# From batch 2 on, attention runs on 64x64 array tiles without the non-causal quarter, one output pass per batch

## Chip, cores and metric

The kernel runs on one core of one Trainium2 chip. The metric is the device time of one execution in microseconds (us). Three runs of the kernel before gave 292.82, 293.95 and 294.68 us; their median is 293.95 us.

## What is computed

The reference, cut to its core (8 batches, 8 heads, 576 positions, head size 64; then 4608 tokens, model size 512, hidden size 2048):

```python
scores = q @ k.transpose(0, 1, 3, 2) / sqrt(64)
gamma = 1 - 2 ** (-5 - head)
D = where(i >= j, gamma ** (i - j), 0)            # causal decay
attn = (scores * D) @ v
x = attn.transpose(0, 2, 1, 3).reshape(4608, 512)
h = x @ w_in
out = gelu_tanh(h) @ w_out
```

## The kernel before

Attention is computed in chunks: each batch has four chunks of 128 positions (512 in all) and a "tail" of 64. For a chunk the kernel computes scores against the same chunk's keys (`score`, line 376), multiplies them by a causal mask (`masks`, L387), and multiplies by the values (`av`, L453). What came before the chunk enters through a running 64x64 state per head: `state` (L399) forms k-transposed times v of a chunk, `scan` (L416) decays and adds it on VectorE (DVE), `spread` (L430) copies the result on ScalarE (ACT) into a block-diagonal weight tile (`tbd`, for the tails `tbt`), and `past` (L436) multiplies that with the queries. The decay factors are put into q and k when these are cast to f16 on GpSimd (POOL, `cast`, L256); v is cast on ACT. `put` (L466) copies a chunk's output from its PSUM bank into `xT`, on ACT.

The second half is an ordinary two-layer network: `up` (L474) makes 512 tokens' hidden activations, 16 steps of four 512-column matmuls, each followed by a GELU on ACT; `prod` (L646) makes the output in 14 steps of eight 256-column matmuls, by seven products of sums of blocks, whose sums are made on DVE (`act_sums` L634, `after` L673). For the last two of the nine token blocks (`WIN`), the hidden layer uses such sums too.

The order is written out by hand. The outer loop at L990 runs over token blocks t = 0 to 8; block t < 8 is the 512 chunk positions of batch t, block 8 holds the eight tails. A block has 30 steps; steps 0 to 15 are `up` and 16 to 29 are `prod`. After step u the events registered with `at(t, u, f)` run, and these are the attention of batch t + 1 and the casts of batch t + 2. Batches 0 and 1 are handled apart: their attention (`score2` L324, `state2` L353, `av2` L365) already uses four 64x64 tiles of the array, on pairs of heads and chunks. From batch 2 on the loop at L946 places, in block t, for batch b = t + 1:

- at step 9 (11 for t = 2, 3): scores and masks of chunks 0 and 1, and in t = 3, 4, 6, 7 those of a pair of tails (`scores`, L917);
- at step 15: `outs` (L928), that is `past`, `av` and `put` of chunks 0, 1 and the tails, with the state of chunks 2, 3; then the scores of chunks 2, 3;
- at steps 17 and 19: the masks of chunks 2, 3; at 16 and 25 `later` (scan and spread) of chunks 2 and 3;
- at step 24: `outs` of chunks 2, 3, with the state of the next batch's chunks 0, 1, whose `later` runs at steps 0 and 1 of the next block.

In t = 1 these stand at steps 16 (state), 21, 23, 25 and 28. The first `up` of block t + 1 reads all four chunks of batch t + 1 in `xT`, so all its `put`s must be done by then. Steps 16 to 23 also hold the casts of batch t + 2 (loop at L966): k and q on POOL, v on ACT, each as its 256 KB load lands, the v of chunk 3 last, at step 23. After them `turn_dma` (L305) transposes k and q by DMA; the transposed tile `tt` is read by the scores of the next block. All loads, transposes and most stores are issued by one queue, that of SyncE (SP), in program order; `load` (L91) issues one DMA for 128 positions of one of q, k, v, and `load_tails` (L81) two DMAs of 64 positions for a pair of tails.

PSUM has eight banks, which the kernel hands out itself: `bank` takes the first of a queue of spare ones, `drop` appends one at the end.

The tile shapes in the profile: `score` multiplies 64 rows by 128 columns of the array, `av` and `state` 128 rows by 64 columns; so two such matmuls (the two heads of a pair) can be in the array at once. `score2`, `state2` and `av2` use 64 rows by 64 columns, four at once.

Of the kernel before, what the change touches and what calls it, by code (L numbers as in the profile page):

```python
# [20 lines left out]
def kernel(  # L21
# [9 lines left out]
    nc = tc.nc  # L31
# [34 lines left out]

    def drop(t):
        spare.append(home.pop(id(t))[0])
# [22 lines left out]
    def load(b, key, c):  # L91
# [8 lines left out]
        else:  # L100
# [3 lines left out]
            )  # L104
        att[b]["raw"][key, c] = t
# [57 lines left out]
    ip = const.tile([128, 4], I32, name="ip")  # L163
    nc.gpsimd.iota(ip[:, 0:2], pattern=[[1, 2]], base=-64, channel_multiplier=2)
    nc.gpsimd.iota(ip[:, 2:4], pattern=[[0, 2]], base=-64, channel_multiplier=1)
# [3 lines left out]
    ps5 = const.tile([128, 8], F32, name="ps5")  # L169
    nc.vector.tensor_copy(out=ps5[:, 0:4], in_=ip)  # L170
    for s, m in ((slice(0, 2), 128.0), (slice(3, 4), 64.0)):
        nc.vector.tensor_scalar(out=ps5[64:128, s], in0=ps5[64:128, s], scalar1=m, scalar2=None, op0=ALU.subtract)
    nc.vector.tensor_scalar(out=ps5[:, 4:8], in0=ps5[:, 0:4], scalar1=-1.0, scalar2=None, op0=ALU.mult)
    lp = const.tile([128, 64], F32, name="lp")
    sc = const.tile([128, 64], F32, name="sc")

    def pairs(x, n):
        return x[:, 16 * n : 16 * n + 16].rearrange("p (n j l) -> p n j l", j=2, l=2)

    lg = lgr.rearrange("p (n l) -> p n l", l=2).unsqueeze(2).to_broadcast([128, 4, 2, 2])  # L180
    for n in range(2):
        pj = ps5[:, 4 * n : 4 * n + 2].unsqueeze(1).unsqueeze(3).to_broadcast([128, 4, 2, 2])
        nc.vector.tensor_tensor(out=pairs(lp, n), in0=lg, in1=pj, op=ALU.mult)
        nc.vector.tensor_tensor(
            out=lp[:, 32 + 16 * n : 48 + 16 * n].rearrange("p (x h) -> p x h", h=8),
            in0=ps5[:, 4 * n + 2 : 4 * n + 4].unsqueeze(2).to_broadcast([128, 2, 8]),
            in1=lgr.unsqueeze(1).to_broadcast([128, 2, 8]), op=ALU.mult,
        )
    lq = lp.rearrange("p (g n x) -> p g n x", g=2, n=2)[:, :, 0]
    nc.vector.tensor_scalar(out=lq, in0=lq, scalar1=math.log(scale), scalar2=None, op0=ALU.add)  # L190
    nc.scalar.activation(out=sc, in_=lp, func=AF.Exp)
    sp = {key: sc[:, 16 * n : 16 * n + 16].rearrange("p (n l) -> p n l", l=2) for n, key in enumerate("qk")}
    sc = sc[:, 32:64].rearrange("p (s h) -> p s h", h=8)
# [7 lines left out]
    cm = const.tile([128, 128], F32, name="cm")  # L201
    tm = const.tile([128, 128], F32, name="tm")
# [11 lines left out]
    def chunk_masks():  # L214
        for m in (cm, tm):
            nc.gpsimd.memset(m, 1.0)
            nc.gpsimd.affine_select(
# [699 lines left out]
    def scores(t, c, tails=None):  # L917
        b = t + 1
        if b < B:
            score(b, c), score(b, c + 1)  # L920
# [163 lines left out]
```

## Time and profile before

| what | value | where from |
|---|---|---|
| median of 3 runs | 293.95 us | runs |
| lowest, highest run | 292.82, 294.68 us | runs |
| profiled execution, first to last instruction | 291.2 us, clock 1.000 | page (it gives no other time of its own) |
| PE matmul starts of block 2 / 3 / 4 / 5 / 6 / 7 | 84.55 / 114.31 / 144.76 / 175.22 / 204.98 / 235.18 us | timeline |
| `ret<-st` masks on DVE, 128x512 | 680 ns, 48 of them | groups |
| `xT<-xs` puts on ACT, 128x512 | 591 ns, 36 of them | groups |

A line of the timeline has the start in us, the length, the engine, the source line, the operation, the output and input tiles, their shapes, the number of instructions merged, and in brackets the idle time before it with what ended it. PE stands for TensorE's matmuls, with array rows and columns in use ahead of the shape. Lengths of matmuls overlap: a small one takes about 0.2 us from start to end, while the next starts a few ns later, so costs on PE are taken from one start to the next.

### The profile page before, as it was taken

Reading aid. Unit: us, or ns where it says so; the run is one execution under the profiler, and the core shown is the slowest. Engines: PE = TensorE matmul, PEld = TensorE weight load, DVE = VectorE, ACT = ScalarE, POOL = GpSimd, SP = SyncE. Lnnn points to the kernel's source line nnn. Section 1 sums busy time; section 2 is a strip of 40 time slices with the busy share of each in tenths; the row PEclk is TensorE's granted clock in tenths of the full one; section 3 lists DMA queues with packets and bytes.
Section 4 is the critical chain, followed back from the end, with each engine's and each line's share of the span. In section 5 each row is a group of like instructions: output and inputs, shape, how many; then the busy total and the mean of one; then the engine's idle time right before and its main releaser. Section 6 shows DMA issues by size and latency. Waiting matters only on the chain.

```text
span 291.2 us, 7390 instructions
## 1 busy us (share of the span) xinstructions
PE 280.6 (96%) x3028; PEld 208.4 (72%) x3028; DVE 204.2 (70%) x409; ACT 169.2 (58%) x320; POOL 100.5 (35%) x129
## 2 busy tenths in 40 slices
PE   6989998999999999999999999999999999999993
PEld 2568886888874687468845884488548887887783
DVE  5797998656864875477548834774489968974863
ACT  5278755896249545965396547664666258507810
POOL 4588869910760085008500740058030000000000
PEclk9999999999999999999999999999999999999999
DMA  7999999999989999999898979999951030003013
GB/s 196 308 367 360 379 294 240 245 235 179 224 168 243 227 204 194 254 229 199 169 234 204 229 155 239 224 202 157 265 106 38 2 144 3 0 24 122 3 36 108
DMA packets 139585, 53.95 MB, mean 185 GB/s; under 512 B 118048, under 2 KB 131360, under 8 KB 139552
## 3 DMA queue, kind: packets, MB, share of 16 engines
q1 hardware_dynamic: 138960, 52.97, 81.4%
q8 instruction: 23, 0.38, 0.5%
q10 hardware_dynamic: 592, 0.52, 0.5%
q14 instruction: 10, 0.08, 0.1%
HBM read 36.70 MB, written 9.44 MB: 158 GB/s over the span
## 4 chain that ended last, share of the span: by engine, by line
PE 81%; DMA 6%; POOL 5%; SPq 4%; DVE 1%; ACT 1%; issue 1%; POOLq 0%
PE hp L480 26%; PE opB L665 13%; PE opA L665 10%; PE opC L665 8%; PE hp L501 5%; DMA ld<-in_moe_w_in_dram 4%; PE hB L574 3%; SPq L96 3%; PE xs L459 3%; PE st L383 3%; POOL w_out_sb L771 2%; DMA ld<-in_q_dram 2%; PE hC L574 2%; PE xs L450 2%; PE opD L665 1%; PE us L408 1%
## 5 line engine op out<-in xcount | busy, mean ns | idle before, releaser
L480 PE MATMUL hp<-xT,w_in_sb 128*128 128x512 f16 x352 | 79.0, 379 | 0.0
L486 ACT ACTIVATE gT<-hp 128x512 f16<-128x512 f32 x88 | 50.1, 600 | 20.7 <-PE hp L480 20.1
L480 PEld LDWEIGHTS <-w_in_sb 128*128 128x128 f16 x352 | 34.0, 98 | 38.2
L665 PEld LDWEIGHTS <-gT 128*128 128x128 f16 x576 | 54.8, 98 | 8.9 <-issue 0.8
L665 PEld LDWEIGHTS <-s 128*128 128x128 f16 x432 | 42.1, 98 | 5.0
L642 DVE TENSOR_TENSOR s<-gT 128x512 f16<-128x512 f16 x36 | 15.6, 434 | 29.8 <-ACT gT L486 23.5
L665 PE MATMUL opA<-w_out_sb,gT 128*128 128x256 f16 x288 | 36.0, 273 | 0.4 <-ACT w_out_sb L771 0.3
L392 DVE TENSOR_TENSOR ret<-st,cm 128x512 f16<-128x512 f32 x48 | 30.1, 680 | 3.6 <-PE st L383 3.6
L469 ACT CAST xT<-xs 128x512 f16<-128x512 f32 x36 | 19.2, 591 | 18.7 <-PE xs L459 15.6
L501 PE MATMUL hp<-xT,w_in_sb 128*128 128x256 f16 x256 | 29.0, 273 | 0.0
L434 ACT CAST tbd<-ws 64x256 f16<-64x256 f32 x48 | 19.3, 403 | 15.3 <-DVE ws L425 14.7
L275 POOL TENSOR_TENSOR ck<-ld,sc 128x512 f16<-128x512 f32 x24 | 25.0, 1040 | 7.7 <-DMA ld<-in_k_dram 7.7
L978 POOL COPY gate<-s 128x1 f16<-128x1 f16 x5 | 0.9, 188 | 76.5 <-DVE s L646 76.5
L275 POOL TENSOR_TENSOR cq<-ld,sc 128x512 f16<-128x512 f32 x24 | 26.2, 1090 | 2.1 <-DMA ld<-in_q_dram 1.8
L501 PEld LDWEIGHTS <-w_in_sb 128*128 128x128 f16 x256 | 24.6, 98 | 3.1
L665 PE MATMUL opB<-wt,gT 128*128 128x256 f16 x224 | 26.8, 273 | 0.0
L262 ACT CAST cv<-ld 128x512 f16<-128x512 f32 x23 | 13.7, 618 | 18.9 <-DMA ld<-in_v_dram 18.8
L508 ACT ACTIVATE gT<-hp 128x512 f16<-128x512 f32 x32 | 18.3, 602 | 3.2 <-PE hp L501 3.0
L679 DVE TENSOR_TENSOR k<-k,opB 128x512 f32<-128x512 f32 x17 | 11.6, 685 | 12.0 <-PE opB L665 11.0
L425 DVE TENSOR_TENSOR ws<-vs,gt 128x256 f32<-128x256 f32 x24 | 18.2, 760 | 1.1
L665 PE MATMUL opB<-wt,s 128*128 128x256 f16 x144 | 17.4, 273 | 0.0
L665 PE MATMUL opC<-wt,s 128*128 128x256 f16 x144 | 17.2, 273 | 0.0
(122 smaller groups left out, 409.1 us busy)
## 6 DMA issues: line engine op xcount, KB each, us to landing
ld<-in_q_dram SPq DMA_DIRECT2D x32, 256.0 KB, 5.3
ld<-in_k_dram SPq DMA_DIRECT2D x32, 256.0 KB, 5.2
ld<-in_v_dram SPq DMA_DIRECT2D x32, 256.0 KB, 5.5
out_dram<-ost SPq DMA_DIRECT2D x16, 512.0 KB, 3.8
ld<-in_moe_w_in_dram SPq DMA_DIRECT2D x16, 256.0 KB, 5.9
ld<-in_moe_w_out_dram SPq DMA_DIRECT2D x16, 256.0 KB, 5.8
lt<-in_k_dram SPq DMA_DIRECT2D x8, 128.0 KB, 4.7
lt<-in_q_dram SPq DMA_DIRECT2D x8, 128.0 KB, 4.3
```

Of the source, the lines that this page charges most:

```text
L275: eng.tensor_tensor(out=dst.rearrange("p (h d) -> p h d", d=D), in0=raw.rearrange("p (h d) -> p h d", d=D), in1=sc[:, s0].unsqueeze(2).to_ ...
L392: nc.vector.tensor_tensor(out=r.rearrange("p (n i) -> p n i", i=128), in0=t.rearrange("p (n i) -> p n i", i=128), in1=(cm if b < PAIR else ...
L425: nc.vector.tensor_tensor(out=w, in0=uc, in1=gt, op=ALU.mult)
L434: cp(out=(tbd[b % 2][r, c, :, r] if c < NC - 1 else tbt[b % NT4][r, :, r]), in_=w[r])
L469: nc.scalar.copy(out=xT[:, g0 : g0 + 2], in_=xs.rearrange("p (n g t) -> p g n t", n=HP, g=2))
L480: nc.tensor.matmul(hp.rearrange("p (g t) -> p g t", t=TL), w_in_sb[:, ct, 128 * fc : 128 * fc + 128], xT[:, o : o + TB // TL, ct, :], star ...
L486: nc.scalar.activation(out=gT[t][:, fc].rearrange("p i n -> p (i n)"), in_=hp, func=AF.Gelu_apprx_tanh)
L501: nc.tensor.matmul(hps[n][:, 256 * x : 256 * x + 256].rearrange("p (g t) -> p g t", t=TL), w_in_sb[:, ct, 128 * (fs[n] + x) : 128 * (fs[n] ...
L508: nc.scalar.activation(out=gT[t][:, f : f + 2, 2 * u : 2 * u + 2, :].rearrange("p f i n -> p f (i n)"), in_=hp.rearrange("p (f n) -> p f n ...
L574: nc.tensor.matmul(pb[:, 256 * i : 256 * i + 256].rearrange("p (g t) -> p g t", t=TL), w(kt, i), x(kt), start=(new and i == kt == 0), stop ...
L642: nc.vector.tensor_tensor(out=s["1"], in0=a21, in1=a22, op=ALU.add)
L665: nc.tensor.matmul(op[tag][:, HD * u : HD * u + HD], lhs(f), rhs[:, f], start=(new and f == 0), stop=(f == NH - 1), skip_group_check=True,)
```

## The change

From batch 2 on, `score` and `av` work on 64x64 tiles of the array. A chunk's scores are cut in halves of 64 keys: the first 64 keys meet all 128 queries, the last 64 keys only the last 64 queries; the quarter in which keys are later than queries is not computed. One pass (`first`) has the matmuls with 128 columns and the other those with 64. To let the two chunks of a pair use different halves of the array in a pass, the halves of k and v of odd chunks are loaded in exchanged order, by two DMAs of 64 positions each, where one DMA of 128 was. The mask tile is 192 wide per pair of heads and a mask instruction handles 384 columns where it handled 512. The tails get the same treatment (`score_tails`, `av_tails`: no scores between the two tails of a pair).

`state` of a batch is made as 64 matmuls on 64x64 tiles in two passes (batch 2: `state_whole`, 32 on 128x64).

The order changes too. The state of all chunks and the scores of chunks 2, 3 are made together at step 15 (`middle`), with the tails' outputs; `later` runs at steps 16, 18, 20, 22; the outputs of all four chunks are made together at step 24 (`outs`; in t = 1 at step 28), with four `put`s after them. Between the passes stands `turn_over`, a four-column matmul on a 64x64 tile into a bank that is taken anew each time: in the program as built, the second and third of them in `outs`, and the first score matmul of the second bank pair in `middle`, wait on PE's own semaphore for the `turn_over` before. Program counts, before and after: 3028 and 3659 matmuls; 24 DMAs more on SP's queue.

The diff, cut (left out: the widened tables of decay factors that the casts use, more buffers for `ret`, and removed lines of the functions printed above):

```diff
+    def turn_over(n):
+        t = ps.tile([128, 512], F32, tag=f"p{n}", name="turn", bufs=1)
+        nc.tensor.matmul(t[0:64, 0:4], ident[0:64, 0:64], ident[0:64, 0:4], start=True, stop=True)
+
...
-        else:
+        elif key == "q" or c % 2 == 0:
             nc.sync.dma_start(
                 out=t.rearrange("p (h d) -> p h d", d=D),
                 in_=src[b, :, 128 * c : 128 * c + 128, :].rearrange("h s d -> s h d"),
             )
+        else:
+            for n in range(2):
+                r0 = 128 * c + 64 - 64 * n
+                nc.sync.dma_start(
+                    out=t[64 * n : 64 * n + 64].rearrange("p (h d) -> p h d", d=D),
+                    in_=src[b, :, r0 : r0 + 64, :].rearrange("h s d -> s h d"),
+                )
...
-    cm = const.tile([128, 128], F32, name="cm")
-    tm = const.tile([128, 128], F32, name="tm")
+    cm = const.tile([128, 192], F32, name="cm")
+    tm = const.tile([128, 64], F32, name="tm")
...
     def chunk_masks():
+        def causal(x, r, i0, n, base):
+            nc.gpsimd.affine_select(
+                out=x[0:r, i0 : i0 + n], in_=x[0:r, i0 : i0 + n], compare_op=ALU.is_ge, fill=0.0, base=base,
+                pattern=[[1, n]], channel_multiplier=-1,
+            )
+
         for m in (cm, tm):
             nc.gpsimd.memset(m, 1.0)
...
+        causal(cm, 128, 0, 64, 64), causal(cm, 128, 64, 128, 64)
+        causal(cm, 64, 0, 128, 0), causal(cm, 64, 128, 64, 0)
+        causal(tm, 128, 0, 64, 64), causal(tm, 64, 0, 64, 0)
 
...
-            s0 = {"q": 0, "k": 2}[key] + (b >= PAIR)
+            s0 = 1 if b >= PAIR else 2 if key == "k" and c % 2 else 0
...
+    def mm(out, lhsT, rhs, start, stop):
+        nc.tensor.matmul(out, lhsT, rhs, start=start, stop=stop, skip_group_check=True)
+
+    def piece(o, first):
+        w = 128 if first else 64
+        return o if first else 1 - o, w, 0 if o == 0 else 64 if first else 128
+
+    def score(b, g):
+        for x in range(2):
+            st = [bank("st") for _ in range(2)]
+            for p in (2 * x, 2 * x + 1):
+                for first in (True, False):
+                    for o in range(2):
+                        h, w, i = piece(o, first)
+                        i += 192 * (p % 2)
+                        for r in range(2):
+                            mm(
+                                st[r][hv(h), i : i + w], att[b]["tt"][hv(r), 0, 4 * (2 * g + o) + p, hv(h)],
+                                tq(b, 2 * g + o, p)[hv(r), 128 - w : 128], True, True,
+                            )
+            att[b]["st", g, x] = st
+
+    def masks(b, g, x):
+        for k, t in enumerate(att[b].pop(("st", g, x))):
+            r = sb.tile([128, 512], F16, tag="ret", name="ret", bufs=8)
+            nc.vector.tensor_tensor(
+                out=r[:, 0:384].rearrange("p (n i) -> p n i", n=2), in0=t[:, 0:384].rearrange("p (n i) -> p n i", n=2),
+                in1=cm.unsqueeze(1).to_broadcast([128, 2, 192]), op=ALU.mult,
+            )
+            drop(t)
+            att[b]["ret"][g, k, x] = r
+
+    def score_tails(b):
         st = [bank("st") for _ in range(2)]
         for p in range(HP):
...
+            for n in range(2):
+                for hl in range(2):
+                    nc.tensor.matmul(
+                        st[hl][hv(n), 64 * p : 64 * p + 64], att[b]["tt"][hv(hl), 0, p, hv(n)],
+                        tq(b, 0, p)[hv(hl), hv(n)], start=True, stop=True,
+                    )
+        for hl, t in enumerate(st):
+            r = sb.tile([128, 512], F16, tag="ret", name="ret", bufs=8)
             nc.vector.tensor_tensor(
-                out=r.rearrange("p (n i) -> p n i", i=128), in0=t.rearrange("p (n i) -> p n i", i=128),
-                in1=(cm if b < PAIR else tm).unsqueeze(1).to_broadcast([128, 4, 128]), op=ALU.mult,
+                out=r[:, 0:256].rearrange("p (n i) -> p n i", n=4), in0=t[:, 0:256].rearrange("p (n i) -> p n i", n=4),
+                in1=tm.unsqueeze(1).to_broadcast([128, 4, 64]), op=ALU.mult,
             )
             drop(t)
-            att[b]["ret"][c, hl] = r
+            att[b]["ret"][hl] = r
 
     def col(c, p, hl):
         return slice(512 * c + 128 * p + 64 * hl, 512 * c + 128 * p + 64 * hl + 64)
 
-    def state(b, *cs):
+    def state(b, first):
         a = att[b]
-        us = bank("us")
-        for n, c in enumerate(cs):
+        if first:
+            a["us"] = [bank("us") for _ in range(2)]
+        for g in range(2):
+            for p in range(HP):
+                for o in range(2):
+                    h, c = hv(piece(o, first)[0]), 2 * g + o
+                    for hl in range(2):
+                        i = 256 * g + 64 * p
+                        mm(
+                            a["us"][o][hv(hl), i : i + 64], a["k"][h, col(c, p, hl)], a["v"][h, col(c, p, hl)],
+                            first and g == p == 0, not first,
+                        )
+        if not first:
+            for c in range(NC):
+                a["U", c] = (a["us"][c % 2], c // 2, c >= 2)
+
+    def state_whole(b):
+        a = att[b]
+        us = [bank("us") for _ in range(2)]
+        for c in range(NC):
             for p in range(HP):
                 for hl in range(2):
...
+                    i = 256 * (c // 2) + 64 * p
+                    mm(us[c % 2][hv(hl), i : i + 64], a["k"][:, col(c, p, hl)], a["v"][:, col(c, p, hl)], True, True)
+            a["U", c] = (us[c % 2], c // 2, c >= 2)
 
...
     def past(b, c):
         xs = bank("xs")
         att[b]["xs", c] = xs
...
+        if c == 0:
+            return
+        for p in range(HP):
+            nc.tensor.matmul(
+                xs[:, 128 * p : 128 * p + 128], tbd[b % 2][:, c - 1, p, :], tq(b, c, p),
+                start=(p == 0), stop=True, skip_group_check=True,
+            )
+
+    def av(b, g, first):
         a = att[b]
         for p in range(HP):
-            for hl in range(2):
+            for o in range(2):
+                h, w, i = piece(o, first)
+                i += 192 * (p % 2)
+                c = 2 * g + o
+                for hl in range(2):
+                    mm(
+                        a["xs", c][hv(hl), 128 * p + 128 - w : 128 * p + 128],
+                        a["v"][hv(h), col(c, p, hl)], a["ret"][g, hl, p // 2][hv(h), i : i + w],
+                        first and c == p == 0, not first,
+                    )
+
+    def past_tails(b, banks):
+        xs = [bank("xs") for _ in range(banks)]
+        att[b]["xs"] = [xs[0], xs[-1]]
+        for n in range(2):
+            for p in range(HP):
+                o = 128 * p + 64 * n
                 nc.tensor.matmul(
...
+                    att[b]["xs"][n][:, o : o + 64], tbt[(b - PAIR + n) % NT4][:, p, :],
+                    tq(b, 0, p)[:, 64 * n : 64 * n + 64],
+                    start=(p == 0 and (n == 0 or banks > 1)), stop=True, skip_group_check=True,
                 )
+
+    def av_tails(b, *ns):
+        a = att[b]
+        for p in range(HP):
+            for n in ns:
+                for hl in range(2):
+                    mm(
+                        a["xs"][n][hv(hl), 128 * p + 64 * n : 128 * p + 64 * n + 64],
+                        a["v"][hv(n), col(0, p, hl)], a["ret"][hl][hv(n), 64 * p : 64 * p + 64], False, True,
+                    )
+
+    def put_tails(b, banks):
+        xs = att[b].pop("xs")
+        g0 = GM + b - PAIR
+        if banks == 1:
+            nc.scalar.copy(out=xT[:, g0 : g0 + 2], in_=xs[0].rearrange("p (n g t) -> p g n t", n=HP, g=2))
+            drop(xs[0])
+            return
+        for n in range(2):
+            nc.scalar.copy(
+                out=xT[:, g0 + n], in_=xs[n].rearrange("p (n g t) -> p g n t", n=HP, g=2)[:, n]
+            )
+            drop(xs[n])
 
     def put(b, c):
         xs = att[b].pop(("xs", c))
-        g0 = 8 * (b % 2) + 2 * c if b < PAIR else GM + b - PAIR
+        g0 = 8 * (b % 2) + 2 * c
         nc.scalar.copy(out=xT[:, g0 : g0 + 2], in_=xs.rearrange("p (n g t) -> p g n t", n=HP, g=2))
         drop(xs)
 
...
+    def middle(b, tails):
+        x = PAIR + tails if tails is not None else None
+        if x:
+            past_tails(x, 1)
+            av_tails(x, 0)
+        state(b, True)
+        turn_over(spare[2])
+        score(b, 1)
+        if x:
+            av_tails(x, 1)
+        state(b, False)
+        if x:
+            put_tails(x, 1)
+
+    def outs(b):
+        for c in range(NC):
+            past(b, c)
+        n = spare.popleft()
+        av(b, 0, True)
+        turn_over(n)
+        av(b, 1, True)
+        turn_over(n)
+        av(b, 0, False)
+        turn_over(n)
+        av(b, 1, False)
+        spare.append(n)
+        for c in range(NC):
+            put(b, c)
+
+    def last_tails(x):
+        past_tails(x, 2)
+        av_tails(x, 0, 1)
+        put_tails(x, 2)
+
+    at(1, 16, lambda: state_whole(2))
     for t in range(1, B):
         b, tl = t + 1, TP.get(t)
...
         if b == B:
+            at(t, 9, lambda x=PAIR + tl: score_tails(x))
+            at(t, 15, lambda x=PAIR + tl: last_tails(x))
             continue
+        s0, s1 = (21, 25) if t == 1 else (11 if t in (2, 3) else 9, 15)
+        at(t, s0, lambda b=b: (score(b, 0), masks(b, 0, 0), masks(b, 0, 1)))
+        if tl is not None:
+            at(t, s0, lambda x=PAIR + tl: score_tails(x))
         if t == 1:
-            at(t, s1, lambda t=t, b=b: scores(t, 2))
+            at(t, s1, lambda b=b: score(b, 1))
+            um, ul, o1 = (25, 25), (17, 18, 19, 20), 28
         else:
...
+            at(t, s1, lambda b=b, tl=tl: middle(b, tl))
+            um, ul, o1 = (17, 19), (16, 18, 20, 22), 24
+        for x, u in enumerate(um):
+            at(t, u, lambda b=b, x=x: masks(b, 1, x))
+        for c, u in enumerate(ul):
+            at(t, u, lambda b=b, c=c: later(b, c))
+        at(t, o1, lambda b=b: outs(b))
 
```

## The prediction

> **What bounds the kernel now.** First the page: how busy each engine is, and the share of the DMA engines over 40 slices.
>
> ```profile
> PE 280.6 (96%) x3028; PEld 208.4 (72%) x3028; DVE 204.2 (70%) x409; ACT 169.2 (58%) x320; POOL 100.5 (35%) x129
> DMA  7999999999989999999898979999951030003013
> ```
>
> PE is the bound: 96% busy, and from 55 us on the list of waits names none of PE. But the second row matters as much: the DMA engines are full until about slice 28 (205 us). So I read PE's timeline for what attention costs (block t = 2), then ACT's at a block's end.
>
> ```profile
> 95.00 0.62 PE L383 MATMUL st<-tt 64*128 64x128 f16 x16
> 95.55 3.63 PE L480 MATMUL hp<-xT,w_in_sb 128*128 128x512 f16 x16
> 99.02 0.39 PE L450 MATMUL xs<-tt,tbd 128*128 128x128 f16 x4
> 99.33 0.64 PE L459 MATMUL xs<-ret,cv 128*64 128x128 f16 x16
> 99.80 0.42 PE L408 MATMUL us<-cv,ck 128*64 128x64 f16 x16
> 100.15 0.62 PE L383 MATMUL st<-tt 64*128 64x128 f16 x16
> 100.71 1.92 PE L665 MATMUL opA<-w_out_sb,gT 128*128 128x256 f16 x16
> ...
> 108.58 0.61 PE L450 MATMUL xs<-tt,tbd 128*128 128x128 f16 x8
> 109.12 0.64 PE L459 MATMUL xs<-ret,cv 128*64 128x128 f16 x16
> 109.59 0.42 PE L408 MATMUL us<-cv,ck 128*64 128x64 f16 x16
> 109.94 0.28 PE L665 MATMUL opA<-w_out_sb,gT 128*128 128x256 f16 x1
> ```
>
> From start to next start, attention takes 0.55 + 1.69 + 1.36 = 3.60 us of the 29.76 us of this block. Two parts hide in it. Single starts in the trace show pairs of matmuls 56 ns apart at 128 columns and 32 ns at 64; and each change of the array's shape shows a gap of about 0.15 us between starts, so about 0.10 more than the pace. One block has 7 such changes.
>
> Batch 1 already runs on four 64x64 tiles, and prices the new form:
>
> ```profile
> 54.23 0.45 PE L359 MATMUL us<-cv,ck 64*64 64x64 f16 x32
> 54.51 0.62 PE L332 MATMUL st<-tt 64*64 64x128 f16 x32
> ```
>
> 32 matmuls of 64 columns take 0.28 us to the next start (single starts: four together every 32 ns), and 32 of 128 columns come by fours every 56 ns. A 64-column four thus costs 57% of a 128-column four, not half.
>
> ACT at the end of block t = 3:
>
> ```profile
> 137.32 0.62 ACT L262 CAST cv<-ld 128x512 f16<-128x512 f32 x1 [1.29 <-DMA ld<-in_v_dram]
> 142.63 0.62 ACT L262 CAST cv<-ld 128x512 f16<-128x512 f32 x1 [4.69 <-DMA ld<-in_v_dram]
> 143.15 1.07 ACT L469 CAST xT<-xs 128x512 f16<-128x512 f32 x2
> ```
>
> The two `put`s had their bank ready at about 140.2 us, but stood on ACT behind the cast of the last v load, which landed at 142.6. They end at 144.2; the next block's first `up` starts at 144.76. In t = 2 it is the same (cast at 112.08, `put`s from 112.60, `up` at 114.31). The slack is 0.5 to 0.7 us.
>
> **The change part by part.** The sum is made against the profiled execution, whose span is 291.2 us; the median of the runs, 293.95, lies 2.75 above it, and I add these 2.75 at the end.
>
> *Scores and outputs.* Per batch, scores were 16 pairs at 56 ns = 0.90 us; they become 8 fours at 56 and 8 at 32 = 0.70. Outputs the same. Together -0.38 us per batch. Skipping a quarter saves 21%.
>
> *State.* 16 pairs at 32 ns become 16 fours at 32: nothing.
>
> *Changes of shape.* From 7 to 6 per block (scores 2, `middle` 2, `outs` 2): -0.10.
>
> *The turn_overs.* No row shows one. Four a block; one uses one tile for four columns. Bounded by the rows: below by 0.01 (the starts inside a four lie 3 to 4 ns apart), above by a change of shape and a full drain each, 0.3. The waits on PE's own semaphore matter more: a 64-column matmul takes 193 ns to its end and DVE follows PE's end by about 45 ns, so the next one can start about 0.25 us after the last. Between the first two lie 4 fours of 128 columns (0.22 us: no wait), between second and third 4 fours of 64 (0.13: wait 0.10), in `middle` 0.18 (wait 0.05). With 0.02 each for the four and 0.02 for refilling the array, I take 0.25 a block; ends 0.05 and 1.2. The Trainium skill (TensorE: Matmul & The Clock Gate, section "Single matmul latency") would give a lone four-column matmul (398 + 4) / 2.4 = 168 ns, an estimate by that page; with 45 ns it would make the waits about 0.03 shorter each.
>
> So a block saves 0.38 + 0.10 - 0.25 = 0.23 us. A pair of tails (t = 3, 4, 6) saves 0.07 more: scores 4 pairs of 128 become 4 fours of 64 (-0.10), outputs 4 pairs of 128 become 8 pairs of 64 (+0.03). In t = 7, tails alone save 0.20.
>
> *Masks.* 680 ns at 512 columns and 420 for a 256-column DVE operation give about 0.55 at 384: DVE gains 1 us a batch, off the path. In t = 6 DVE runs without a gap from 218.7 to 230.6, and two more scans (1.2 us) now stand there before the one that `past` needs. Counted through, that scan ends at 229.7 and its spread (0.82) at 230.5, `past` of chunk 3 wants it at about 230.4: I take 0.2, ends 0 and 0.8.
>
> *Loads.* 24 more DMAs on SP, which holds all loads and transposes. Behind them wait the casts on ACT and POOL, then the transposes. The nearest row is the tails' loads, the same two DMAs of 64 positions: an issue takes 0.63 us against 0.57 for a whole load when nothing holds it, but the queue is 4 to 5 us ahead of the engines, and what counts is landing. In t = 3 and 5 the tails' pairs landed 1.09 us apart on average, whole loads mostly 1.0 to 1.2. I take 0; ends -0.1 and +0.2 per pair, 16 pairs until the last v of block 3. POOL's new masks (8 instructions for 5 of 0.14 to 0.31, so +0.8) end 2 us before the transposes at 62.15: nothing.
>
> *Four puts at the block's end.* ACT's `put`s follow each other by 0.48, the last takes 0.58. Four end 2.02 us after the first starts. Two of four used to be done at step 15.
>
> Now block by block, as the shift of the next block's first matmul:
> - t = 1: state +0.25 (all four chunks at once), scores -0.20, `outs` at step 23 gone (-1.29): `outs` begins at 81.06, `past` of 12 takes 0.76, `av` with its turns 0.93. The first bank is complete at 82.7, the `put`s end at 84.72. PE alone would be ready at 83.7. It waits 1.05: start 84.75 instead of 84.55, +0.2.
> - t = 2: PE ready at 84.75 + 29.76 - 0.23 = 114.28; ACT: 112.60 + 2.02 = 114.62, and 0.05 to PE. Start 114.67, +0.36.
> - t = 3: PE ready at 144.82; ACT 143.15 + 2.02 + 0.05 = 145.2. Start 145.2, +0.44.
> - t = 4: ACT's last v cast is at 171.58, four `put`s end at 174.2, `up` at 175.4: no wait. -0.30: +0.14. t = 5: -0.23: -0.09. t = 6: +0.26 (half of its batch's state was made in t = 5), -0.30, +0.2: +0.07. t = 7: -0.20: -0.13.
>
> The span is 291.07, the time **293.8 us**: no change. What PE gains up to block 4 is spent waiting for the loads, which are full.
>
> **The rivals.**
> 1. *Loads slip (slower).* If a split pair lands 0.2 us later than a whole load, the v of block 3 lands 3.2 us later, and block 4 starts 3.6 late; after it 0.57 is gained: a span of 294.3, 297.0 us. One per cent is passed from 0.19 us a pair. For it: ten tenths of DMA. Against: the tails' pairs. 12%.
> 2. *Turn_overs drain the array (slower).* At 0.3 each plus waits a block loses 0.7 instead of gaining 0.23: with six such blocks and the waits for ACT within them about +4 us, 298. Against: 64x64 stages with waits of PE on itself run without gaps today. 6%.
> 3. *Matmuls cost by the piece (slower).* If a 64-column matmul on a 64x64 tile took what one on 128x64 takes (0.35 us / 16 = 22 ns), the 128 of a batch would take 2.8 us, not 1.0: +10.7 us, 304. Against it the row at 54.23: 9 ns each. 2%. The Trainium skill (TensorE: Matmul & The Clock Gate, "Wait — 56ns, not 53.3ns?") has a floor of about 25 ns from start to start however few columns: that would speak against this change, +13 us by its figure; here the trace disagrees, with starts 3 to 4 ns apart on different tiles.
> 4. *The gain arrives (faster).* Turns at 0.05 a block and no waiting for `put`s: -0.7 in t = 1, -0.45 or -0.55 in t = 2 to 5, -0.25, -0.2: -3.1, so 290.8. It needs the last v a microsecond earlier than today's 142.6; nothing in the change moves it. 6%.
>
> **The numbers.** Forecast 74%, its own range 292.4 to 295.6: below with turns at 0.05 (-0.9 from the span) and the 0.6 by which runs differ; above with turns at 0.6 a block and the loads at +0.05 a pair. For 8 in 10 the range reaches to 1 and 4 in part: 292.1 to 297.0. One per cent (2.9 us) is about what a measurement here can tell. Faster by more: 5%, rival 4. Slower by more: half of 1, and 2 and 3: 14%. Within: 81%.
>
> **What would show it.** Blocks 2, 3 and 4 begin at 84.8, 114.7 and 145.2, PE idle ahead of the first `hp` for 1.05, 0.4 and 0.4 us, released by the ACT `put`; four `put`s in a row behind the last v cast. The scores' 32 matmuls take 0.45 us to the next start, not 0.55; `outs` 1.7. A block without a wait is 0.2 us shorter (5: 29.5). It is wrong if the last v lands later than 142.6 by a microsecond, or if the turns show gaps of over 0.1 us.

## The result: 3.2% slower

The changed kernel takes 302.21 us (median of five runs, 302.0 to 304.78); the kernel before took 292.93 us beside it (five runs, 292.34 to 294.68). The ratio is 1.0318, 95% interval 1.0274 to 1.0361. The forecast was 293.8 us. Of `e1`, `g1` and `h1` below, some executions (one of four, five of ten, one of twelve) were over 1.5% longer than the fastest of the same kernel, and the ratios leave those out; the median of all ten of `g1` is 298.33 us.

The page of the changed kernel, in the profiled execution (span 302.9 us, its own time 304.78): how busy each engine is, then the granted clock and the DMA share over 40 slices.

```profile
PE 282.9 (93%) x3659; PEld 207.8 (69%) x3659; DVE 195.3 (64%) x410; ACT 171.3 (57%) x321; POOL 101.5 (34%) x132
...
PEclk9999999999999999599999999999999999999999
DMA  7999999999999999999999979999992020003013
```

PE is busy for 2.3 us more than before (282.9 against 280.6) while the span is 11.7 us longer: most of the loss is waiting, and part of the 2.3 is one slice at a lower clock. DMA is full from slice 2 to slice 30 with one dip (slice 24), where before it also dipped at slices 12, 20 and 22 and fell off a slice earlier.

PE's timeline around blocks 2 and 3 of the changed kernel; the brackets hold the idle time and what ended it:

```profile
86.44 10.52 PE L570 MATMUL hp<-xT,w_in_sb 128*128 128x512 f16 x48 [0.93 <-ACT xT L559]
98.47 0.54 PE L396 MATMUL st<-tt 64*64 64x128 f16 x32 [1.52 <-DMA tt<-cq]
...
112.90 0.40 PE L502 MATMUL xs<-tt,tbd 128*128 128x128 f16 x4 [0.77 <-ACT tbd L494]
...
122.77 13.04 PE L570 MATMUL hp<-xT,w_in_sb 128*128 128x512 f16 x48 [3.97 <-ACT xT L559]
```

Three waits in block 2 (1.52 for the transposed queries, 0.77 for a spread, 3.97 ahead of block 3) were not there before. After the longest one, the same 48 matmuls that take 10.52 us take 13.04: single starts are 427 ns apart for the first 5 us and 216 ns after that.

ACT at the end of block 2 of the changed kernel:

```profile
111.51 0.62 ACT L278 CAST cv<-ld 128x512 f16<-128x512 f32 x1 [2.84 <-DMA ld<-in_v_dram]
...
115.45 0.62 ACT L278 CAST cv<-ld 128x512 f16<-128x512 f32 x1 [2.61 <-DMA ld<-in_v_dram]
...
120.16 0.62 ACT L278 CAST cv<-ld 128x512 f16<-128x512 f32 x1 [3.37 <-DMA ld<-in_v_dram]
120.68 2.04 ACT L559 CAST xT<-xs 128x512 f16<-128x512 f32 x4
```

The cast of the same v, and the `put`s behind it, in the kernel before:

```profile
112.08 0.62 ACT L262 CAST cv<-ld 128x512 f16<-128x512 f32 x1 [2.98 <-DMA ld<-in_v_dram]
112.60 1.06 ACT L469 CAST xT<-xs 128x512 f16<-128x512 f32 x2
```

ACT waits for v after v. The last one lands 6.4 us later than before (120.08 against 112.06, less 1.58 us by which this execution was already later at the first `opE` matmul, near 40 us), and the four `put`s stand behind its cast.

By blocks, from one start to the next; "before" and "after" are lengths in us, the last two columns the difference as predicted and as it came:

| stretch | before | after | predicted | measured |
|---|---|---|---|---|
| first `opE` to block 2 | 45.33 | 45.64 | +0.2 | +0.31 |
| block 2 | 29.76 | 36.33 | +0.16 | +6.57 |
| block 3 | 30.45 | 32.78 | +0.08 | +2.33 |
| block 4 | 30.46 | 30.25 | -0.30 | -0.21 |
| block 5 | 29.76 | 29.75 | -0.23 | -0.01 |
| block 6 | 30.20 | 31.48 | +0.16 | +1.28 |
| block 7 to the end | 56.02 | 55.87 | -0.20 | -0.15 |

These sum to 10.1 us; the rest of the 11.7 is the 1.58 us up to the first `opE`. That start varies from 38.5 to 40.8 us over the profiles of this study, with kernels of either kind among the early ones, so it is not put down to the change, though the four latest (from 40.0 us on) are all versions of the changed kernel. Blocks 2 and 3 hold 8.9 us of the 10.1.

### The profile page after: what moved, and what is told of

Read it like the earlier page. It is cut to its first block, busy times and chain, and to the rows that moved or that the text cites. A ratio compares the mean times of both kernels' runs of the same rounds, so it can differ in the third digit from the quotient of the medians.

```text
span 302.9 us, 8711 instructions
## 1 busy us (share of the span) xinstructions
PE 282.9 (93%) x3659; PEld 207.8 (69%) x3659; DVE 195.3 (64%) x410; ACT 171.3 (57%) x321; POOL 101.5 (34%) x132
## 5 line engine op out<-in xcount | busy, mean ns | idle before, releaser
L570 PE MATMUL hp<-xT,w_in_sb 128*128 128x512 f16 x352 | 81.5, 388 | 4.9 <-ACT xT L559 4.9
L576 ACT ACTIVATE gT<-hp 128x512 f16<-128x512 f32 x88 | 52.5, 597 | 36.4 <-PE hp L570 35.9
L732 DVE TENSOR_TENSOR s<-gT 128x512 f16<-128x512 f16 x36 | 16.6, 462 | 48.7 <-ACT gT L576 40.0
L591 PE MATMUL hp<-xT,w_in_sb 128*128 128x256 f16 x256 | 29.9, 273 | 1.1 <-POOL w_in_sb L861 0.8
L291 POOL TENSOR_TENSOR ck<-ld,sc 128x512 f16<-128x512 f32 x24 | 26.5, 1102 | 12.4 <-DMA ld<-in_k_dram 12.4
L420 DVE TENSOR_TENSOR ret<-st,cm 128x384 f16<-128x384 f32 x48 | 23.7, 547 | 4.7 <-PE st L396 4.7
L598 ACT ACTIVATE gT<-hp 128x512 f16<-128x512 f32 x32 | 18.4, 602 | 4.3 <-PE hp L591 4.0
L559 ACT CAST xT<-xs 128x512 f16<-128x512 f32 x32 | 16.6, 596 | 7.4 <-PE turn L69 4.1
L734 DVE TENSOR_TENSOR gT<-gT 128x512 f16<-128x512 f16 x36 | 17.5, 487 | 0.0
L733 DVE TENSOR_TENSOR s<-s,gT 128x512 f16<-128x512 f16 x36 | 16.6, 461 | 1.2
```

Of the source, the lines that this page charges most:

```text
L291: eng.tensor_tensor(out=dst.rearrange("p (h d) -> p h d", d=D), in0=raw.rearrange("p (h d) -> p h d", d=D), in1=sx[key][:, s0].unsqueeze(2 ...
L420: nc.vector.tensor_tensor(out=r[:, 0:384].rearrange("p (n i) -> p n i", n=2), in0=t[:, 0:384].rearrange("p (n i) -> p n i", n=2), in1=cm.u ...
L559: nc.scalar.copy(out=xT[:, g0 : g0 + 2], in_=xs.rearrange("p (n g t) -> p g n t", n=HP, g=2))
L570: nc.tensor.matmul(hp.rearrange("p (g t) -> p g t", t=TL), w_in_sb[:, ct, 128 * fc : 128 * fc + 128], xT[:, o : o + TB // TL, ct, :], star ...
L576: nc.scalar.activation(out=gT[t][:, fc].rearrange("p i n -> p (i n)"), in_=hp, func=AF.Gelu_apprx_tanh)
L591: nc.tensor.matmul(hps[n][:, 256 * x : 256 * x + 256].rearrange("p (g t) -> p g t", t=TL), w_in_sb[:, ct, 128 * (fs[n] + x) : 128 * (fs[n] ...
```

## The experiments

All ratios are to runs of the kernel before on the same chip; a median is of the executions that its ratio is from (`e1`, `g1`) or of all.

| label | kernel | us (median) | ratio, 95% interval |
|---|---|---|---|
| e1_whole_loads | after, one DMA per load | 298.20 | 1.0130 (1.0059 to 1.0201) |
| e2_before_split | before, odd k and v in two contiguous halves | 298.82 | 1.0176 (1.0123 to 1.0228) |
| e3_late_v_cast | after, cast of the last v behind the `put`s | 299.70 | 1.0222 (1.0167 to 1.0276) |
| e4_before_split_by_heads | before, odd k and v in two halves of the heads | 293.56 | 1.0013 (0.9985 to 1.0042) |
| g1_whole_loads_masks_late | e1, chunk masks at step 12 of block 1 | 294.70 | 1.0071 (1.0033 to 1.0109) |
| g2_swap_in_cast | after, one DMA per load, halves exchanged in the cast, masks late | 296.68 | 1.0118 (1.0086 to 1.0151) |
| g3_keep_clock | after, 16 idle matmuls ahead of block 3 | 301.60 | 1.0277 (1.0238 to 1.0316) |
| g4_before_split_interleaved | before, odd k and v as even and odd positions | 294.25 | 1.0025 (0.9997 to 1.0052) |
| h1_swap_late_v | g2, cast of the last v behind the `put`s | 294.71 | 1.0031 (1.0004 to 1.0057) |
| h2_before_late_v | before, with that late cast | 293.21 | 1.0000 (0.9978 to 1.0022) |
| h3_swap_late_v_outs_moved | h1, outputs moved in blocks 1 and 6 | 296.97 | 1.0116 (1.0084 to 1.0148) |
| h4_swap_late_v_scans_early | h1, scans of block 6 earlier | 293.82 | 1.0021 (0.9994 to 1.0047) |

### The split loads alone, three ways (e2, e4, g4)

The theory after the result: a load in two DMAs of 64 positions costs DMA time, and all else follows from late loads. Rivals: it is the number of DMAs that costs (SP's issues), or the loads are late because the rest of the change delays what frees their buffers. Three kernels put nothing but split loads into the kernel before, with the halves cut in different ways.

```diff
+        else:
+            for n in range(2):
+                r0 = 128 * c + 64 * n                                   # e2
+                nc.sync.dma_start(
+                    out=t[64 * n : 64 * n + 64].rearrange("p (h d) -> p h d", d=D),
+                    in_=src[b, :, r0 : r0 + 64, :].rearrange("h s d -> s h d"),
+                )
...
+                    out=t[:, 256 * n : 256 * n + 256].rearrange("p (h d) -> p h d", d=D),     # e4
+                    in_=src[b, 4 * n : 4 * n + 4, 128 * c : 128 * c + 128, :].rearrange("h s d -> s h d"),
...
+                    out=t[n::2].rearrange("p (h d) -> p h d", d=D),     # g4
+                    in_=src[b, :, r0 + n : r0 + 128 : 2, :].rearrange("h s d -> s h d"),
```

> The kernel before with one edit: k and v of odd chunks are loaded by two DMAs of 64 positions each, halves in their plain order, output unchanged. Theory A: the loads slip as in the changed kernel; two puts behind the last v cast of block 2 end about 5 us later, so 298 to 301 us. Theory B or C alone: 293 us.

> The kernel before, k and v of odd chunks loaded by two DMAs of 128 positions and four heads each: as many DMAs and packets as in the split by positions, but each writes all 128 partitions. If a DMA costs by its count: as slow as the split by positions, 298 to 301 us. If it is the 64 partitions that are slow: 293 us.

> The kernel before, k and v of odd chunks loaded by two DMAs of 64 positions each, one taking the even and one the odd positions, so that each reaches partitions all over the 128. If a DMA is slow because its 64 partitions lie in one half: about 293 us, like the split by heads. If it is slow because it has only 64 partitions or half the rows: 298 to 299 us, like the split into halves.

The contiguous halves alone cost 1.76%, 5.2 us. The other two cuts have exactly as many DMAs and cost 0.13% and 0.25%, intervals that hold 1. So it is not the count. Landings of the twelve loads of a batch, from the first k to the last v, in the traces:

| kernel | batch 3, us | batch 4, us | extra per split pair (of 4) |
|---|---|---|---|
| before | 13.66 | 13.99 | |
| e4, halves by heads | 13.22 | 14.31 | -0.11, +0.08 |
| g4, even and odd positions | 13.60 | 13.98 | 0.0, 0.0 |
| e2, contiguous halves | 15.34 | 16.06 | +0.42, +0.52 |
| after, contiguous halves exchanged | 16.16 | 17.02 | +0.62, +0.76 |
| g2 (below), whole loads, halves exchanged in the cast | 14.57 | 15.38 | no pairs; +0.9 and +1.4 in all |

In batches 5 to 7 the loads of `e2` take 15.62, 15.63 and 15.82 us, those of the kernel before 15.68, 13.14 and 14.78: -0.02, +0.62 and +0.26 a pair, and 0.36 on the average of the five batches. Not all of the lateness in the changed kernel is the split. Less what each execution was already late at the first `opE`, its last v of block 2 lands 6.4 us later than before and that of `e2` 5.0, but with whole loads it is still 1.1 (`e1`), 1.3 (`h1`) and 2.3 us (`g2`).

In these runs a load in two DMAs of 64 positions costs nothing when each writes every second of the 128 partitions, and time when each writes the lower or the upper half. The Trainium skill has a rule for this in "SBUF — State Buffer" (section "Door 1: The DMA port swizzle"): partitions 0 to 63 reach only 8 of 16 ports; and by the section "Can I just issue two DMAs to hit both halves?" two DMAs, one per half, serialize. By its rule every second partition reaches all 16. These rows agree with all three; they show the cost, not the ports themselves. The cuts also differ in what they read (64 positions in a row, every second one, or half of the heads), and no run changes the partitions alone.

And the kernel before shows two of the three new waits of the changed one, once it has such loads (PE's timeline of `e2`):

```profile
97.03 0.62 PE L390 MATMUL st<-tt 64*128 64x128 f16 x16 [1.25 <-DMA tt<-cq]
...
119.21 11.84 PE L487 MATMUL hp<-xT,w_in_sb 128*128 128x512 f16 x48 [2.70 <-ACT xT L476]
```

Here PE waits for the transposed queries in block 2, and for the `put`s ahead of block 3, at the same two places as in the changed kernel, with no 64x64 tile of the change in it.

### The change without split loads (e1, g1, g2)

`e1` undoes the split only, so odd chunks meet the wrong half of their keys; `g1` also moves `chunk_masks` from step 0 to step 12 of block 1; `g2` is the full computation, the halves exchanged when they are cast.

```diff
-        elif key == "q" or c % 2 == 0:
+        elif True:                                                      # e1, g1, g2
...
-    at(1, 0, chunk_masks)
+    at(1, 12, chunk_masks)                                              # g1, g2
...
+            for o, i in halves:                                         # g2
+                if eng is nc.scalar:
+                    eng.copy(out=dst[o], in_=raw[i])
...
```

> The changed kernel with one DMA of 128 positions for every load: the halves of odd chunks of k and v are not exchanged, so the attention of odd chunks is computed from the wrong keys; every instruction on the engines stays. Theory A (the split loads slip, 0.6 to 0.75 us a pair, and everything else follows): last v of block 2 lands about 6 us earlier, the wait ahead of block 3 shrinks from 4.0 to about 0.4 us, no slice at half clock, 294 us. Theory B (the work that was added on TensorE, turn_overs and shape changes, costs it): the time stays at 302. Theory C (four puts behind the last v cast cost it even with whole loads): 297 to 299.

> The changed kernel with one DMA for every load (odd chunks' halves not exchanged, so their attention is computed from the wrong keys) and with the masks made on POOL behind the casts of batch 2 (step 12 of block 1 instead of 0). Theory A+ (the split loads, and in the run with whole loads a DVE operation that stands for 4 us beside POOL casts without a gap, are all that is wrong): the 2.65 us wait at 57 us goes and the time is what was forecast for the change, 293.5 to 294.5 us. If the new order on TensorE and ACT costs by itself: 296 or more.

> As the last, but with the right keys: whole loads, and the halves of odd chunks of k and v exchanged by the casts, which take two instructions of 64 partitions each (2 more a batch on POOL, 2 more on ACT). Theory A+: 294 to 296 us, the rest being POOL's two casts of 1 us in a chain that leads to the transposes. If the casts cost as much as the split did: 298 to 302.

Whole loads take away more than half of the loss: from 1.0318 to 1.0130 (`e1`) and 1.0118 (`g2`); the 1.0071 of `g1` stands on five of its ten executions. With `g2`, which computes everything, that is 2.0%, 5.9 us, near the 5.2 us that `e2` put in. No one of the three reaches the times that theory A had for them, and the 298.20 of `e1` is what theory C had; but its profile shows no wait ahead of block 3.

`e1` has a wait of its own, 2.65 us for a mask in block 1. DVE in `e1`:

```profile
54.68 0.42 DVE L482 TENSOR_TENSOR vs<-us,ws 128x256 f32<-128x256 f32 x1 [2.60 <-PE us L375]
55.14 4.68 DVE L485 TENSOR_TENSOR ws<-vs,gt 128x256 f32<-128x256 f32 x1
```

The second operation takes 0.42 to 1.31 us at its other places in these kernels. It ended at 59.82, 0.3 us after a train of eight casts on POOL that ran from 51.49 to 59.53 us without a gap. The new masks (six instructions, 49.98 to 51.51) stand just ahead of that train, and with the masks later (`g1`, `g2`) the long operation is gone (0.95 and 1.28 us). But in the kernel before the same eight casts run from 50.98 to 59.21 us without a gap too, and the operation at 55.2 takes 1.13 us beside them. So why it takes 4.68 us in `e1` stays open; it is one profile. After the wait for it the granted clock of `e1` is 0.5 from 60.8 to 64.2 us, which adds to its loss.

`g1` and `g2` still wait ahead of block 3, for the `put`s. PE in `g1` (in the profiled execution, 300.38 us), then ACT in `g2`:

```profile
118.08 13.48 PE L570 MATMUL hp<-xT,w_in_sb 128*128 128x512 f16 x48 [3.75 <-ACT xT L559]
```

```profile
114.30 1.25 ACT L281 CAST cv<-ld 64x512 f16<-64x512 f32 x2 [2.97 <-DMA ld<-in_v_dram]
115.57 2.05 ACT L563 CAST xT<-xs 128x512 f16<-128x512 f32 x4
```

In `g2` the bank contents were complete at about 110.6 us, but the four `put`s start at 115.57, behind the last v. PE then waits 2.59 us ahead of block 3 (117.67). That is the mechanism of theory C, and the next edit takes it out.

### The cast of the last v behind the puts (e3, h1, h2)

```diff
         for u, (key, c) in zip(ut, ent):
+            if b > NPE + 1 and key == "v" and c == 3:
+                u = 25
```

> The changed kernel, the ACT cast of a batch's last v load moved behind the four puts (step 25 instead of 23), loads split as they are. Theory A: loads land as late as in the changed kernel, but the wait ahead of block 3 (4.0 us) and the slow clock behind it (2.5 us) go: about 296 us; the 1.5 us wait for the transposed q in block 2 stays. Theory B: 302.

> Whole loads, halves exchanged in the cast, chunk masks made later (the kernel that took 296.68 us, ratio 1.0118), and now the cast of the v of chunk 3 stands at step 25, behind the four puts, where it stood at 23 (batches 4 and later). Theory (the four puts stand on ACT behind a late v, and that is most of what is left): the 2.59 us that PE waited ahead of block 3 go, and nothing takes their place, as DMA has only whole loads: about 294.1 us, ratio 1.003. Rival (the loads are late as a whole, and the wait only moves on to the transposed queries or the next block's start): the same sum of waits of PE under other names, 296 us or more, ratio 1.010.

> The kernel before with the same cast of v at step 25. PE there has no wait ahead of a block, so both theories expect no change, ratio 0.998 to 1.002; if the cast at step 23 held something that the list of waits does not show, the kernel before gains too, and the two versions must be compared with that.

With split loads (`e3`) it gains about 1%, to 299.70 us and not to the expected 296, and the loads' lateness shows elsewhere: PE waits 2.1 us in four places for spreads and 1.7 in two for the transposed queries. With whole loads (`h1`) the time is 294.71 and the ratio 1.0031, 0.9 points below `g2` and as the theory had it. PE and ACT in `h1`:

```profile
86.03 10.52 PE L574 MATMUL hp<-xT,w_in_sb 128*128 128x512 f16 x48 [0.93 <-ACT xT L563]
115.70 10.52 PE L574 MATMUL hp<-xT,w_in_sb 128*128 128x512 f16 x48
```

```profile
111.73 2.05 ACT L563 CAST xT<-xs 128x512 f16<-128x512 f32 x4
113.65 0.63 ACT L829 COPY ost<-opA 128x512 f32<-128x512 f32 x1
114.14 1.25 ACT L281 CAST cv<-ld 64x512 f16<-64x512 f32 x2
```

The `put`s now run when their banks are ready, the v cast follows at 114.14, and block 3 starts without a wait. The kernel before gains nothing from the same edit (`h2`, 1.0000): its two `put`s had slack.

### What is left: block 6 (h3, h4)

In `h1`, blocks 2 to 5 are shorter than before by 0.09, 0.19, 0.21 and 0.09 us, and block 6 is longer by 1.29 (31.49 against 30.20). In the changed kernel itself, PE in block 6:

```profile
239.63 0.61 PE L502 MATMUL xs<-tt,tbd 128*128 128x128 f16 x8
240.66 0.40 PE L502 MATMUL xs<-tt,tbd 128*128 128x128 f16 x4 [0.41 <-ACT tbd L494]
240.99 0.42 PE L396 MATMUL xs<-ret,cv 64*64 64x128 f16 x16
241.84 0.19 PE L69 MATMUL turn<-ident 64*64 64x4 f16 x1 [0.44 <-DVE vs L482]
```

From start to start, the twelve `past` take 1.36 us where block 5 has 0.76, and the first part of `av` 0.85 where it has 0.25: 1.2 us for two waits, the first for the spread of chunk 2's scan, the second for the bank that the last scan gives back.

`h3` moves the outputs (block 1: step 27; block 6: step 26), `h4` the scans instead:

```diff
+            um, ul, o1 = (25, 25), (17, 18, 19, 20), 27                         # h3, t = 1
+            um, ul, o1 = (17, 19), (16, 18, 20, 22), 26 if t == 6 else 24       # h3
...
+            if t == 6:                                                          # h4
+                ul = (16, 17, 18, 20)
```

> As the first kernel of this call, and the outputs of block 1 one step earlier (27) and those of block 6 two steps later (26). Theory (what is left is a wait of 0.93 us ahead of block 2 for the four puts, and about 1.2 us in block 6 for a scan that DVE makes late): both go, 2.0 us less than the first kernel, about 292.1 us, ratio 0.996. Rival (they are waits for something that stays late, the scan's spread or the masks of chunks 2 and 3): block 1 then waits in its outputs for a mask, block 6 ahead of block 7 for the puts, and the time is that of the first kernel.

> Whole loads, halves exchanged in the cast, late v cast (the kernel that took 294.71 us, ratio 1.0031), and in block 6 the scans of chunks 2 and 3 stand at steps 18 and 20 instead of 20 and 22, so ahead of seven sums of weights in DVE's order. Theory (block 6 is longer by 1.3 us because two scans more stand in a DVE queue without a gap, and past and the turn_over wait for the last two): the two waits of 0.43 and 0.44 us in block 6 go, with the slow starts around them 1.2 us, about 293.5 us, ratio 0.999. Rival (DVE is full there, and whatever is moved ahead makes the evictions of the output banks late, as moving the outputs did, which cost 2.24 us ahead of a product): PE waits for the eviction instead, the time is that of the first kernel or more, ratio 1.003 to 1.006.

`h3` fails. The wait of 0.93 ahead of block 2 goes, but two of 0.34 come (a spread at 109.39, the tails' transpose at 155.14), and block 6 gets longer, 34.04 us against 31.49 in `h1`. PE and DVE in block 6 of `h3`:

```profile
233.35 1.03 PE L759 MATMUL opB<-wt,gT 128*128 128x256 f16 x8 [2.24 <-DVE k L773]
234.22 1.26 PE L506 MATMUL xs<-tt,tbd 128*128 128x128 f16 x12
```

```profile
231.82 0.42 DVE L486 TENSOR_TENSOR vs<-us,ws 128x256 f32<-128x256 f32 x1
232.27 0.43 DVE L489 TENSOR_TENSOR ws<-vs,gt 128x256 f32<-128x256 f32 x1
232.61 0.68 DVE L773 TENSOR_TENSOR k<-k,opB 128x512 f32<-128x512 f32 x1
```

The eviction of `opB` stands behind the last scan in DVE's queue; with the outputs later, PE reaches the next `opB` product sooner and waits 2.24 us for that eviction instead. Then the granted clock is 0.5 from 234.45 to 237.87 us: the outputs take 2.77 us from start to start, where block 5 of the changed kernel has 1.79. The other five executions show a clock of 0.999 or 1.000 and a median of 296.32 us, so most of the loss is not the clock. The theory failed, and the rival named other waits (for a mask, for the `put`s); it was right in that something stays late, here DVE. In `h4` the waits in the outputs are gone:

```profile
226.92 1.91 PE L759 MATMUL opB<-wt,gT 128*128 128x256 f16 x16 [0.24 <-DVE k L773]
...
229.53 0.83 PE L506 MATMUL xs<-tt,tbd 128*128 128x128 f16 x12
230.30 0.42 PE L400 MATMUL xs<-ret,cv 64*64 64x128 f16 x16
230.54 0.16 PE L69 MATMUL turn<-ident 64*64 64x4 f16 x1
```

Two smaller ones stand in their place (0.24 for an eviction, as the rival had it, and about 0.2 ahead of the `opB` at 232.41), and block 6 takes 30.85 us: half of the 1.29 is back, not all as the theory had it. The ratio, 1.0021, is 0.1 points below that of `h1`, less than their intervals can tell.

### The clock (g3)

Sixteen 512-column matmuls into an unused bank keep PE busy ahead of block 3 of the changed kernel.

> The changed kernel with 16 idle matmuls of 512 columns on TensorE ahead of block 3, into a spare bank that nothing reads. They take 3.5 us of the 4.0 us in which it waits there. Theory: of the loss ahead of block 3 about 2.5 us is the slow clock after the wait, so the first 48 hp matmuls take 10.5 us instead of 13.0 and the time falls by 1.5 to 2.5, to about 300. If the clock is not what stretches them: 302 to 303.

PE in `g3`:

```profile
118.61 3.62 PE L1067 MATMUL fill<-w_in_sb,ident 128*128 128x512 f16 x16
122.29 1.02 PE L570 MATMUL hp<-xT,w_in_sb 128*128 128x512 f16 x4
```

The clock stays at 1.000 and the 48 matmuls take 10.52 us again, so the idle time made them slow. But the medians differ by 0.6 us only (301.60 against 302.21), within what the two intervals leave: block 5 then starts with a wait of 0.66 us for the `put`s, which the changed kernel does not have. As long as the loads are late, a faster PE arrives early at the next wait. One of the five executions of the changed kernel itself had a granted clock of 1.000 and took 302.39 us, no less than the median, so the half clock alone does not set the time.

## Why the prediction was wrong

The failed step is "I take 0; ends -0.1 and +0.2 per pair", under *Loads*. In `e2` a split pair costs 0.42 and 0.52 us in the two batches whose loads set the new waits, over twice the upper end, and 0.36 on the average of batches 3 to 7. Behind these pairs the last v of block 2 lands 5.0 us later in `e2`, and in the changed kernel 6.4, of which 1.1 to 2.3 come with whole loads too. Rival 1 had the mechanism and the sign, with its own threshold (one per cent from 0.19 us a pair), and 12% for it.

The row that I priced it by misled. The tails' pairs are contiguous halves too, and those of t = 3 and 5 landed 1.09 us apart on average, like whole loads. Those of t = 2, in the same trace, landed 1.38 us apart and were left out. And three such pairs follow one another ahead of the transposes, with no whole load behind them, and none of those rows says what a pair does to the loads behind it. In `e2` a pair of halves in the middle of a batch takes 1.61 us from the landing ahead of it (k of chunk 1 of batch 4: 103.96 to 105.57) where before a whole load takes 1.21. That the issues on SP cost nothing was right: `e4` and `g4` add as many DMAs.

The other steps, in their order:

- *Scores, outputs, state, turn_overs.* Mostly right. In block 5 of the changed kernel (PE's timeline):

```profile
194.53 0.54 PE L396 MATMUL st<-tt 64*64 64x128 f16 x32
195.00 5.35 PE L570 MATMUL hp<-xT,w_in_sb 128*128 128x512 f16 x24
...
209.38 0.83 PE L502 MATMUL xs<-tt,tbd 128*128 128x128 f16 x12
210.14 0.42 PE L396 MATMUL xs<-ret,cv 64*64 64x128 f16 x16
210.39 0.16 PE L69 MATMUL turn<-ident 64*64 64x4 f16 x1
...
210.66 0.16 PE L69 MATMUL turn<-ident 64*64 64x4 f16 x1
...
210.92 0.16 PE L69 MATMUL turn<-ident 64*64 64x4 f16 x1
...
211.17 1.05 PE L755 MATMUL opA<-w_out_sb,gT 128*128 128x256 f16 x8
```

  The scores take 0.47 us (predicted 0.45), the outputs 1.79 (1.7). Between the second and the third `turn_over` lie 0.26 us for matmuls that take 0.13: a wait of 0.13, predicted 0.10. The block without any wait saves 0.01 us here and 0.09 in `h1`, predicted 0.23. The outputs' `av` takes 1.03 us from the first matmul to the next `opA`, where 8 fours at 56 ns, 8 at 32 and one change of shape would make 0.80 (the other change lies ahead of the first matmul); `middle` in `h1` takes 1.14 where 16 fours at 32 ns, 4 at 56, 4 at 32 and one change make 0.96. So the `turn_over`s cost 0.41 (0.23 and 0.18) for 0.25, and these 0.16 are about what the block's saving falls short. Rivals 2 and 3 are out.
- *Four puts at the block's end.* Right for block 2: 0.93 us of waiting for 1.05. For block 3 the term was right in kind and drowned by the late v: 3.97 for 0.4. `h1` shows that the order, `put`s behind the last v cast, is worth 0.9%.
- *t = 6.* "I take 0.2, ends 0 and 0.8" for the late scan: 1.2 us came. The scan's spread was counted, but not the second wait, of a `turn_over` for the bank that the last scan frees.
- *Masks on DVE, POOL's masks.* The 384-column masks take 547 ns on average, for 0.55 us predicted. That POOL's masks cost nothing held in the changed kernel; in `e1`, with whole loads, PE waits 2.65 us behind the DVE operation of 4.68 us, which is gone once the masks are made later.
- *Rival 4.* With whole loads and the late cast the gain does not arrive either: `h1` and `h4` end at 1.0031 and 1.0021. Half a per cent of gain would have been seen. Where no wait interferes a block gains 0.1 to 0.2 us, and the wait ahead of block 2 and DVE in block 6 take it back.

So of the 9.3 us between the medians, by steps of the ratio times 293 us, 5.9 go with the split loads (1.0318 to 1.0118), 2.5 with the `put`s behind the last v cast (to 1.0031), and 0.3 with the scans of block 6 (to 1.0021); what remains, 0.6 us, is within the interval. These are steps between versions: `g2` also exchanges the halves in the casts and makes the masks later. No version here beats the kernel before.

What stays open: why the tails' pairs mostly land as fast as whole loads, and why even whole loads take longer in `g2` than before. The gap between an exchanged pair (0.62 and 0.76) and a plain one (0.42 and 0.52) may go with the latter: measured against the whole loads of `g2`, an exchanged pair costs 0.40 and 0.41 us, in one profile each.

## What to carry to other kernels

Price a changed load by what it does to the loads behind it in a full queue, and look at which partitions it writes, not only at its bytes and the number of DMAs: here half of the partitions in one piece was dear, and every second one free. Before work is gathered at the end of a stage, see what its engine's queue holds ahead of it: four `put`s behind one late load cost 0.9%, and one moved cast gave it back. A gain of 0.1 or 0.2 us a stage on PE is worth having only after the waits around it have slack.

## What the runs showed of the hardware

- DMA: in a full queue, 128 KB into 64 contiguous partitions, twice, took 0.42 and 0.52 us longer than 256 KB into 128 (`e2`, batches 3 and 4; 0.36 on the average of batches 3 to 7); into every second partition, twice, it took no longer (`g4`).
- DVE beside POOL: an operation with two inputs in SBUF, 0.42 us at its shortest, took 4.68 us, until a train of POOL casts without a gap had ended (`e1`). Beside such a train in the kernel before it took 1.13 us, so the train alone is not the cause.
- Clock: at a granted clock of 1.000, 512-column matmuls start 216 ns apart, at 0.5 they start 427 ns apart. The clock was 0.5 for 6.8 us from 2.3 us into the wait of 3.97 us (changed kernel), and for 3.4 us in or after waits of 2.65 (`e1`), 2.70 (`e2`) and 2.24 us (`h3`); after 2.59 us (`g2`) it stayed at 1.000. So the length of the wait alone does not decide. The Trainium skill (TensorE: Matmul & The Clock Gate, section "What's actually happening") has the clock halved after an idle window of about 3.4 us, and full again after as long a busy one. The halved clock agrees, and 3.97 us does; that 2.24 to 2.70 us were enough does not.
